# Two used-up phase places hold the transform constants of the last chunk's first four ticks

## The chip, the core and the metric

The kernel runs on one core of a Trainium2 chip. A core has a matrix engine (PE, which multiplies, with its weight loads PEld), a vector engine (DVE), a scalar engine (ACT), a general engine (POOL) and a sync engine (SP), each with its own queue of instructions, and 16 DMA engines that move data between the device memory and the on-chip memory. The metric is device time in microseconds (us) of one execution. Times of a profile count from the start of the profiled span.

## The reference

One layer over a sequence of 2048 positions with 640 features, all in float32. A vector `c` gives shifts, scales and gates (`mod`). A normalised, modulated copy of the input goes through a long convolution whose filter is the real part of a sum of 128 damped complex exponentials per feature; its gated result is added to the input, and a gated feed-forward part follows.

```python
h = _layernorm(x) * (1 + ca) + sa
# _A_ref, per feature d:
P = jnp.exp(logdA[:, :, None] * l[None, None, :])
K = jnp.einsum("dn,dnl,dn->dl", Cc, P, dB).real
Kf = rfft(pad(K)); Uf = rfft(pad(u))
y = irfft(Uf * Kf)[:L] + u * Dskip
x = x + ga * y
h = _layernorm(x) * (1 + cb) + sb
x = x + gb * ((silu(h @ w1) * (h @ w3)) @ w2)
```

## The kernel before

The convolution is done as a two-stage transform written as matmuls, over five chunks of 128 features (`NDC` = 5). For each chunk the filter's tables are made in eight steps of 16 features (`SD`), 40 steps in all: POOL makes integer phases (`phases`, tile `ph`, two steps at a time), ACT takes their cosine and sine in place, ACT makes exponentials (tables `A`), DVE multiplies (`E`, `A`), PE sums them (`kgen`) and does the filter's first stage (`k_stage1`), and `k_out` writes the result to `uk`.

The second stage works on groups. A chunk has eight groups of four frequencies, so there are 40 group steps, called ticks. Tick k, from 10 (`LAG`) to 49, belongs to chunk (k - 10) // 8 and group (k - 10) % 8; the last chunk has ticks 42 to 49. A tick runs these pieces, each a function of chunk and group:

- `stage2`: loads a constant tile `s2` (256 KB) with SP, unless one was loaded ahead and lies in the dictionary `ahead`; 16 matmuls multiply it with the input's and the filter's first stage in `uk` into the PSUM tile `p2`.
- `k_copy` (ACT, tile `kc`), `products` (DVE, tiles `T` and `p2` itself) and `sums` (DVE, tile `Y`) make the complex product.
- `inverse1`: loads a constant tile `i1` (256 KB) in the same way and runs 16 matmuls into `pz`. It comes one tick later than `stage2`, behind the next tick's `stage2`.
- `z_store`: ACT copies `pz` to `zt`, and a DMA writes it to the device memory (`zs`). For the last chunk `z_last` stores each group by itself, and behind groups 5 and 7 reloads the last columns.

`s2`, `i1`, `kc`, `T`, `Y` and `zt` are tiles of the pool `fp` with two places each. In the trace `s2` and `i1` have the names `s` and `i`, `p2` is `p`. A tile's load waits until the last reader of its place is done. The order of ACT, DVE and PE is written out by hand in the list `ROUND` as far as tick 42 (in a round that starts at 4 r, `iv+4` is `inverse1` of tick 4 r + 4); the loop over `tk` (line 981) does the rest. SP's instructions aren't pinned: the scheduler sets them in its own order, except where `tc.issue_after` puts one behind another on the same engine. `i1_last` (line 735) keeps the latest `i1` load for that.

In ticks 47 to 50 `x_part` (line 822) brings the first four row blocks back from `zs`, through loads that POOL issues (`z_load`, line 785), and DVE adds them to the input. Behind the last `i1` load go the first feed-forward weights (line 1001) and two blocks of the input. Then the pools of the convolution are closed and the feed-forward part begins with `x_first` (line 1050); it starts with matmuls on zeros (`idle`) that only keep PE busy.

A phase tile `ph` takes 8,576 bytes in each partition and the pool `tp` has three places for it. `tp` is closed at tick 41, and the pool `xp` of the feed-forward part is opened in its room. 20 phase tiles are made, the last for steps 38 and 39.

The lines behind which an `i1` or `s2` load stands are 685 and 691; those two names are also the key with which a tile is looked up in `ahead`.

Of the kernel before, what the change touches and what calls it, by code (L numbers as in the profile page):

```python
# [9 lines left out]
F32 = mybir.dt.float32  # L10
F32R = mybir.dt.float32r
I32 = mybir.dt.int32
# [5 lines left out]
P = 128  # L18
# [5 lines left out]
NDC = D // DC  # L24
SD = 16
# [9 lines left out]
NPG = NPH + NG - 1  # L35
# [57 lines left out]
def bc(ap, axis, n):  # L93
    v = ap.unsqueeze(axis)
    shape = list(v.shape)
    shape[axis] = n
    return v.broadcast_to(shape)
# [18 lines left out]
def tile_kernel(ctx: ExitStack, tc: tile.TileContext, a):  # L116
    nc = tc.nc
# [22 lines left out]
    def keep(ins):  # L140

        return tc.keep_in_program_order(ins) if in_order[0] else ins
# [22 lines left out]
    ssm = ExitStack()  # L165
# [7 lines left out]
    one4 = kp.tile([P, 1], F32, name="one4")  # L173
    cT = kp.tile([P, KD], F32, name="cT")
    uk = kp.tile([P, 3, NA, DC], F32, name="uk")

    psS = ssm.enter_context(tc.tile_pool(name="psS", bufs=1, space=PSUM))

# [2 lines left out]
    tp = tabs.enter_context(tc.tile_pool(name="tp", bufs=2, reuse_waits="tile"))  # L181
# [251 lines left out]
    def late_load(i):  # L433

        late[i] = w_load(xw[:, :KD * WC].rearrange("p (k c) -> p k c", k=KD), 1920 + i * WC)
# [108 lines left out]
    ph, cs, AA, EC, PK, K1 = {}, {}, {}, {}, {}, {}  # L544
# [39 lines left out]

    def phases(s):
        sl = slice(s * SD, s * SD + 2 * SD)
        p = tp.tile([P, 2 * SD, NPG], I32, name="ph", bufs=3)
        hold = tc.keep_in_program_order if 0 < s < 4 else keep
        b0 = NA - 8
        base = p[:, :, b0:NA]  # L590
        hold(G.tensor_tensor(p[:, :, b0:], bc(thi[:, sl], 2, NPG - b0), bc(iota, 1, 2 * SD), op=OP.mult))
        keep(G.tensor_tensor(base, base, bc(phi[:, sl], 2, 8), op=OP.add))
        keep(G.tensor_tensor(p[:, :, :b0].rearrange("p k (g j) -> p k g j", j=8), bc(base, 2, NG - 1),
                             bc(p[:, :, NPH:], 3, 8), op=OP.add))
        ph[s] = p[:, :, :NPH]
# [84 lines left out]
    ahead = {}  # L680
# [7 lines left out]
    def inverse1_load(g):  # L688

        i1 = fp.tile([P, 2, 2, P], F32, name="i1")  # L690
        i1_last[0] = nc.sync.dma_start(i1, a["i1"][:, g * 2:g * 2 + 2])
        return i1

    def stage2(ch, g):
        s2 = ahead.pop((ch, g, "s2"), None)
        if s2 is None:
            s2 = stage2_load(g)
        kn = 1 + ch % 2

        n = ch * 8 + g  # L700
        p2 = psS.tile([P, 2, 2, 2 * DC], F32, name="p2", tag="B" if n > NS - 12 and n % 2 else "A", bufs=1)
        for pi in range(2):
            for c in range(2):
                for par in range(2):
                    f = g * 4 + pi * 2 + par
                    keep(PE.matmul(p2[par * 64:par * 64 + 64, pi, c, :], s2[:, pi * 2 + par, c * 64:c * 64 + 64],
                                   uk[:, 0:kn + 1:kn, f, :], start=True, stop=True, tile_position=(0, par * 64)))
        Pq[ch, g] = p2
        if g % 2 == 1 and ch + 1 < NDC:
            u_load(ch + 1, g // 2)  # L710
# [24 lines left out]
    i1_last = [None]  # L735

    def inverse1(ch, g):
        i1 = ahead.pop((ch, g, "i1"), None)
        if i1 is None:
            i1 = inverse1_load(g)  # L740
        Y = Yq.pop((ch, g))
        if g % 2 == 0:
            Zq[ch] = psS.tile([P, 2, 4, DC], F32, name="pz", tag="Z", bufs=1)
        pz = Zq[ch]
        for pi in range(2):
            for c in range(2):
                for par in range(2):
                    r = slice(par * 64, par * 64 + 64)
                    ins = keep(PE.matmul(pz[:, par, (g % 2) * 2 + pi, :], i1[r, pi, c, :], Y[r, pi, c, :],
                                         start=(c == 0), stop=(c == 1), tile_position=(par * 64, 0)))  # L750
        return ins
# [33 lines left out]
    def z_load(z, j, ks, q=nc.sync, b0=0):  # L785

        nb = z.shape[1]
        for k in ks:
            hh = int(k > 1)
            kk = k - 2 * hh  # L790
            q.dma_start(z[hh * 64:hh * 64 + 64, :, kk * DC:kk * DC + DC],
                        zsv[:, 4 * j + b0:4 * j + b0 + nb, k])
# [7 lines left out]
    def z_tile():  # L800
        z = tz.tile([P, SD, 3, NA], F32, name="A")
        return z.rearrange("p k s b -> p (k s b)").rearrange("p (b d) -> p b d", b=4)
# [15 lines left out]
    def x_load(j):  # L818
        xe.append(xw[:, j * D:(j + 1) * D])
        nc.sync.dma_start(xe[j], a["x"][j * P:(j + 1) * P, :])  # L820
# [21 lines left out]
    def conv_part(fn):  # L842
        return lambda k: fn((k - LAG) // 8, (k - LAG) % 8)

    parts = {"PH": phases, "AB": absph, "CO": cosine, "SI": sine, "PA": lambda k: exp_fast((k,)), "XA": fast,
             "PQ": lambda k: exp_slow((k,)), "XQ": slow, "E1": real1, "E2": real2, "A1": imag1, "A2": imag2,
             "kg": kgen, "K": k1evac, "pt": k_stage1, "uk": k_out}
# [5 lines left out]
    def do(name, k):  # L853

        lo, hi = (LAG, LAG + 8 * NDC) if name in conv else (0, NS)
        if name in by_two and k % 2:
            return None
        if front[0]:
            assert (name, k) not in done and lo <= k < hi, (name, k)
        if (name, k) in done or not lo <= k < hi or (name == "zt" and k % 2 == 0 and k < LAG + 8 * NDC - 8):  # L860
            return None
        done.add((name, k))
        return (conv if name in conv else parts)[name](k)
# [20 lines left out]
    def u_first(i):  # L884

        u_load(0, i)
        if i == 0:
            ahead[0, 1, "s2"] = stage2_load(1)
            for g in range(2):
                ahead[0, g, "i1"] = inverse1_load(g)  # L890
# [45 lines left out]
    for word in FRONT:  # L936
        name, k = word[:2].rstrip("+"), int(word[len(word[:2].rstrip("+")):])
# [25 lines left out]
    for rnd in range(NS // EB):  # L963
        if 2 <= rnd < 7:
            late_load(rnd - 2)
        for word in ROUND:
            name, k = word[:2].rstrip("+-"), EB * rnd + int(word[len(word[:2].rstrip("+-")):])
            if name in pieces:
                if 2 <= rnd < 7:
                    pieces[name](rnd - 2)  # L970
                continue
            do(name, k)
            if name == "E1" and 30 <= k < 38 and k % 2 == 0:
                x_load((k - 30) // 2)

            if name == "kg" and 36 <= k < 40:
                early.append((None, z_tile()))
                z_load(early[-1][1], k - 36, range(3), q=nc.gpsimd)
    in_order[0] = False

    for tk in range(NS + 1, LAG + 8 * NDC + 2):
# [13 lines left out]
        i = tk - 1 - LAG - 8 * NDC + 8  # L995
# [190 lines left out]
    ahead = {(0, n): w for n, w in first_w.items()}  # L1186
# [272 lines left out]
    for pair in range(2):  # L1459
# [4 lines left out]
        side = []  # L1464
# [8 lines left out]
        if pair == 0:  # L1473
            tiles = []
            power = x_first(tiles)
            for k in range(KD):
# [12 lines left out]
            side = [lambda: mid(0), lambda: (mid(1), mid(2)), lambda: mid(3), lambda: None,  # L1489
                    lambda: turn(4, 0, 2), lambda: turn(3, 1)]  # L1490
# [106 lines left out]
```

## Time and profile before

| | |
|---|---|
| time, median of 3 runs | 943.76 us (942.69 to 943.88) |
| the profiled execution | 944.3 us, of which the span 942.3 us |
| PE busy | 874.9 us (93%) |
| DVE busy | 699.1 us (74%) |
| ACT busy | 541.6 us (57%) |
| POOL busy | 268.4 us (28%) |
| moved by DMA | 140.66 MB, 149 GB/s on average |
| first and last `stage2` | 123.5 and 360.9 us |
| loads of `s2` and of `i1` | 40 each, 256 KB, issued by SP |

The stretch that matters here lies between 300 us (tick 36) and 420 us (the feed-forward part under way). In the timeline a row has its start, its length, the engine, the line, the operation, output and input with their shapes, a count, and in brackets the idle time of the engine ahead of it with what ended it. Most instructions have line 110, that of the wrapper which records them, so they are told apart by their tiles. A row of PE with x16 and `p<-uk,s` is one tick's `stage2`, one with `pz<-Y,i` its `inverse1`. SPq rows are DMA issues; they show when a load was issued, not when it landed.

### The profile page before, as it was taken

The numbers are of one execution on the slowest core, as the hardware profiler recorded it, in microseconds if no ns is written. First come the engines' busy times: TensorE is split into PE (matmuls) and PEld (weight loads), VectorE is DVE, ScalarE is ACT, GpSimd is POOL, SyncE is SP. The second block draws the span as 40 slices with busy tenths as digits, with TensorE's granted clock in tenths as the row PEclk, the third lists the DMA queues.
The fourth block names the chain that finished last, engine by engine and source line by source line (L and its number), as shares of the span: only waits on it lengthen the run. The fifth ranks groups of instructions, "written<-read, shape, count | busy, mean of one in ns | idle before, by whom it ended". The sixth has DMA issues, their size and how long they took to land.

```text
span 942.3 us, 19918 instructions
## 1 busy us (share of the span) xinstructions
PE 874.9 (93%) x7950; PEld 665.5 (71%) x7950; DVE 699.1 (74%) x1209; ACT 541.6 (57%) x747; POOL 268.4 (28%) x277
## 2 busy tenths in 40 slices
PE   3788989999988888999999999999999999999997
PEld 2445566666666655678888886678888888888885
DVE  5899899999999857686666655677876666664674
ACT  6989889999999432474333322465643333323332
POOL 3333544554444011223222201320332222200341
PEclk9777689999999999999999999999999999999999
DMA  9664476576666786952111227946312322123352
GB/s 273 208 221 177 150 204 211 175 214 192 180 201 179 206 254 201 274 191 85 56 57 56 56 71 204 268 143 197 117 51 57 112 56 57 56 85 97 102 199 77
DMA packets 103279, 140.66 MB, mean 149 GB/s; under 512 B 20276, under 2 KB 62388, under 8 KB 103188
## 3 DMA queue, kind: packets, MB, share of 16 engines
q1 hardware_dynamic: 92452, 113.45, 39.8%
q10 hardware_dynamic: 8432, 18.22, 6.4%
q0 software_dynamic: 2304, 7.74, 2.5%
q8 instruction: 62, 1.02, 0.5%
q14 instruction: 29, 0.24, 0.1%
HBM read 107.92 MB, written 31.46 MB: 148 GB/s over the span
## 4 chain that ended last, share of the span: by engine, by line
PE 66%; DVE 15%; ACT 6%; DMA 5%; SPq 4%; issue 3%; POOL 0%; DVEq 0%; ACTq 0%; POOLq 0%
PE ps L110 49%; PE p L110 6%; SPq L110 3%; PE pt L110 3%; PE pz L110 3%; DVE A L110 2%; PE pk L110 2%; DVE E L110 2%; DVE u L110 2%; PE pa L110 2%; DVE uk L110 1%; DMA s<-in_s_dram 1%; DVE st L110 1%; ACT cs L110 1%; ACT A L110 1%
## 5 line engine op out<-in xcount | busy, mean ns | idle before, releaser
L110 DVE TENSOR_TENSOR s<-ps,s 128x512 f32<-128x512 f32 x138 | 94.9, 688 | 83.0 <-PE ps L110 82.7
L110 ACT CAST gh<-rw 128x640 fp32r<-128x640 f32 x87 | 63.3, 728 | 130.0 <-PE ps L110 90.8
L110 DVE TENSOR_TENSOR gl<-rw,gh 128x640 fp32r<-128x640 f32 x87 | 77.3, 888 | 71.1 <-ACT gh L110 71.1
L110 POOL TENSOR_TENSOR S<-rw 128x256 f32<-128x256 f32 x46 | 36.6, 797 | 234.7 <-DVE S0l L110 158.1
L110 PE MATMUL p<-uk,s 128*64 128x256 f32 x640 | 80.9, 396 | 15.1 <-DVE Y L110 3.4
L110 PE MATMUL ps<-xA,gh 128*128 128x512 f32 x280 | 87.6, 391 | 0.4 <-ACT xA L110 0.4
L110 PE MATMUL ps<-gh,uh 128*128 128x512 f32 x224 | 87.8, 392 | 0.0
L110 PE MATMUL ps<-gl,uh 128*128 128x512 f32 x224 | 87.4, 390 | 0.0
L110 POOL TENSOR_TENSOR ph<-thi,iota 128x1376 int32<-128x1376 int32 x20 | 51.2, 2560 | 115.8 <-DVE A L110 94.6
L110 DVE TENSOR_TENSOR E<-A,cs 128x1024 f32<-128x1024 f32 (+1 forms) x80 | 81.0, 1024 | 2.5 <-PE pk L110 1.9
L110 PE MATMUL ps<-gh,ul 128*128 128x512 f32 x208 | 81.1, 390 | 0.0
L110 PEld LDWEIGHTS p<-uk,s 128*64 128x64 f32 x640 | 46.3, 140 | 39.3 <-DVE Y L110 5.7
L110 ACT ACTIVATE A<-pa 128x1024 f32<-128x1024 f32 (+1 forms) x80 | 64.2, 814 | 9.4 <-PE pa L110 8.9
L110 PEld LDWEIGHTS ps<-xA,gh 128*128 128x128 f32 x280 | 52.3, 188 | 12.9 <-issue 1.2
L110 DVE TENSOR_TENSOR A<-A,ph 128x1024 f32<-128x1024 f32 x40 | 54.2, 1358 | 0.8
L110 PE MATMUL ps<-xA,gl 128*128 128x512 f32 x140 | 54.5, 389 | 0.0
L110 PE MATMUL pt<-s,K 128*64 128x128 f32 x640 | 46.8, 291 | 5.4 <-ACT uk L110 5.4
L110 PE MATMUL pz<-Y,i 64*128 64x128 f32 x640 | 46.9, 286 | 2.4 <-DVE Y L110 1.6
L110 PEld LDWEIGHTS ps<-gh,uh 128*128 128x128 f32 x224 | 42.2, 188 | 9.4 <-DVE h L110 0.6
L110 PEld LDWEIGHTS pz<-Y,i 64*128 64x128 f32 x640 | 39.3, 188 | 13.3 <-issue 8.9
L110 PEld LDWEIGHTS ps<-gl,uh 128*128 128x128 f32 x224 | 42.2, 188 | 9.0
L110 PEld LDWEIGHTS pt<-s,K 128*64 128x64 f32 x640 | 37.1, 145 | 14.1 <-ACT uk L110 8.7
(214 smaller groups left out, 2156.5 us busy)
## 6 DMA issues: line engine op xcount, KB each, us to landing
rw<-in_w_dram ACTq DMA_DIRECT2D x44, 320.0 KB
us<-u SPq DMA_DIRECT2D x16, 640.0 KB
s<-in_s_dram SPq DMA_DIRECT2D x40, 256.0 KB
i<-in_i_dram SPq DMA_DIRECT2D x40, 256.0 KB
rw<-in_wg_dram SPq DMA_DIRECT2D x31, 320.0 KB
rw<-in_wu_dram SPq DMA_DIRECT2D x28, 320.0 KB
uk<-us SPq DMA_DIRECT2D x16, 512.0 KB
zs<-zt SPq DMA_DIRECT2D x16, 512.0 KB
```

The lines of the kernel that those rows point to most:

```text
L110: ins = fn(*args, **kw)
```

## The change

The phase tiles get a pool of their own, `php`, with the same three places, on the side of the memory that stays until the convolution is over; so the phase places are no longer part of `tp`. After the `inverse1` of ticks 36, 37, 38 and 39 a new function `last_pair` loads the `s2` and the `i1` of the last chunk's groups 0, 1, 2 and 3 (ticks 42 to 45) and leaves them in `ahead`. Groups 0 and 1 share one phase tile, groups 2 and 3 the next; four constants of 512 floats each fill 8,192 of its 8,576 bytes in a partition. `tc.issue_after` puts each pair on SP behind the newest `i1` load. `stage2` and `inverse1` of ticks 42 to 45 then find their constants in `ahead` and take no place of `s2` and `i1` in `fp`. Ticks 46 to 49 load as before. The same bytes are loaded in all, and no computing instruction is added or left out.

```diff
--- before.py
+++ after.py
@@ -173,6 +173,10 @@
     one4 = kp.tile([P, 1], F32, name="one4")
     cT = kp.tile([P, KD], F32, name="cT")
     uk = kp.tile([P, 3, NA, DC], F32, name="uk")
+    php = ssm.enter_context(tc.tile_pool(name="php", bufs=3, side="right", reuse_waits="tile"))
+
+    def phase_tile():
+        return php.tile([P, 2 * SD, NPG], I32, name="ph")
 
     psS = ssm.enter_context(tc.tile_pool(name="psS", bufs=1, space=PSUM))
 
@@ -584,7 +588,7 @@
 
     def phases(s):
         sl = slice(s * SD, s * SD + 2 * SD)
-        p = tp.tile([P, 2 * SD, NPG], I32, name="ph", bufs=3)
+        p = phase_tile()
         hold = tc.keep_in_program_order if 0 < s < 4 else keep
         b0 = NA - 8
         base = p[:, :, b0:NA]
@@ -690,6 +694,19 @@
         i1 = fp.tile([P, 2, 2, P], F32, name="i1")
         i1_last[0] = nc.sync.dma_start(i1, a["i1"][:, g * 2:g * 2 + 2])
         return i1
+
+    kept = []
+
+    def last_pair(g):
+
+        if g % 2 == 0:
+            kept.append(phase_tile().rearrange("p k b -> p (k b)").bitcast(F32))
+        for i, (name, src, n) in enumerate((("s2", a["s2"], 4), ("i1", a["i1"], 2))):
+            o = (g % 2 * 2 + i) * 4 * P
+            v = kept[-1][:, o:o + 4 * P]
+            v = v.rearrange("p (f c) -> p f c", f=4) if i == 0 else v.rearrange("p (f h c) -> p f h c", f=2, h=2)
+            nc.sync.dma_start(v, src[:, g * n:g * n + n])
+            ahead[NDC - 1, g, name] = v
 
     def stage2(ch, g):
         s2 = ahead.pop((ch, g, "s2"), None)
@@ -970,6 +987,9 @@
                     pieces[name](rnd - 2)
                 continue
             do(name, k)
+            if name == "iv" and 36 <= k < 40:
+                with tc.issue_after(i1_last[0].ins):
+                    last_pair(k - 36)
             if name == "E1" and 30 <= k < 38 and k % 2 == 0:
                 x_load((k - 30) // 2)
 
```

## The prediction

> **What bounds the kernel now.** I read the page's chain first (DMA carries only 5% of it), then the chain in order of time, to see where that DMA sits. Between 300 and 370 us, in the last ticks of the convolution, two of its links are loads of the forward constant s2 (named `s<-in_s_dram`), and each has matmuls waiting at its end. In the chain of waits the columns are start, length and what:
>
> ```profile
> 332.02 6.59 DMA s<-in_s_dram
> ...
> 338.75 3.25 PE p L110 x16
> ...
> 345.33 5.39 DMA s<-in_s_dram
> ```
>
> The same stretch in the timeline of PE. `p<-uk,s` is `stage2` of a tick (16 matmuls), `pz<-Y,i` is `inverse1` of the tick before. Counting back from the last one (tick 49), the row at 338.75 is `stage2` of tick 43, 343.35 tick 44, 346.31 tick 45, 350.77 tick 46, 353.74 tick 47, 357.30 tick 48.
>
> ```profile
> 335.28 1.16 PE L110 MATMUL pz<-Y,i 64*128 64x128 f32 x16
> 338.75 3.25 PE L110 MATMUL p<-uk,s 128*64 128x256 f32 x16 [2.31 <-DMA s<-in_s_dram]
> 341.93 1.48 PE L110 MATMUL pz<-Y,i 64*128 64x128 f32 x16
> 343.35 1.95 PE L110 MATMUL p<-uk,s 128*64 128x256 f32 x16
> ...
> 346.31 1.95 PE L110 MATMUL p<-uk,s 128*64 128x256 f32 x16
> 349.12 1.16 PE L110 MATMUL pz<-Y,i 64*128 64x128 f32 x16 [0.85 <-DMA i<-in_i_dram]
> 350.77 1.95 PE L110 MATMUL p<-uk,s 128*64 128x256 f32 x16 [0.49 <-DMA s<-in_s_dram]
> ...
> 353.74 1.95 PE L110 MATMUL p<-uk,s 128*64 128x256 f32 x16
> ...
> 357.30 1.95 PE L110 MATMUL p<-uk,s 128*64 128x256 f32 x16
> ```
>
> An undisturbed tick is 346.31 - 343.35 = 2.96 us. Three stalls on constants stand in these rows: 2.31, 0.85 and 0.49 us. The first has an aftermath: tick 43 takes 3.25 us where the others take 1.95, and the inverse behind it 1.48 where the others take 1.16. The table by windows tells why. Its columns are PE, PEld, DVE, ACT and POOL busy, then the granted clock, the DMA share and GB/s:
>
> ```profile
> 335.00:340.00 5.00, 2.69 (x28) 1.93 (x26) 2.14 (x4) 1.60 (x2) 0.00 (x0) 0.92 0.99 355
> 340.00:345.00 5.00, 5.00 (x42) 3.25 (x38) 2.14 (x4) 1.17 (x2) 2.44 (x4) 0.74 0.38 116
> ```
>
> The stall lies where the DMA share is 0.99, and behind it the granted clock falls to 0.74. So ticks 43 to 46 are bound by their constants, twice directly and once through the clock.
>
> **The change, part by part.** Every load of a constant goes into one of two places, so the load for tick k waits until tick k-2 has used the place. SyncE's timeline shows it:
>
> ```profile
> 300.31 0.33 SPq L691 DMA_DIRECT2D i<-in_i_dram  x1
> ...
> 309.54 0.53 SPq L685 DMA_DIRECT2D s<-in_s_dram  x1
> 312.21 0.33 SPq L691 DMA_DIRECT2D i<-in_i_dram  x1
> ...
> 316.81 0.33 SPq L691 DMA_DIRECT2D i<-in_i_dram  x1
> ...
> 321.22 0.58 SPq L685 DMA_DIRECT2D s<-in_s_dram  x1
> ...
> 328.58 0.33 SPq L685 DMA_DIRECT2D s<-in_s_dram  x1
> ...
> 342.03 0.33 SPq L685 DMA_DIRECT2D s<-in_s_dram  x1
> ```
>
> The load at 342.03 goes out as tick 43 ends (338.75 + 3.25 = 342.0), and tick 45 at 346.31 uses it without a wait: it landed within 4.28 us. The one at 345.33 took 5.39. I keep these two as the ends for a load's time.
>
> *The eight moved loads.* The s2 and i1 of ticks 42 to 45 (256 KB each) now go out behind the i1 loads of ticks 36 to 39, the first at 300.31 and the last at 316.81. They need two phase places. The last readers of those are DVE's `A<-ph` of tables 35 and 37:
>
> ```profile
> 298.87 0.69 DVE L110 SCALAR_TENSOR_TENSOR A<-ph,A 128x512 f32<-128x512 f32 x1
> ...
> 310.00 0.69 DVE L110 SCALAR_TENSOR_TENSOR A<-ph,A 128x512 f32<-128x512 f32 x1
> ```
>
> Table 35 ends at 299.56, ahead of the first pair (300.31). Table 37 ends at 310.69, ahead of the i1 load of tick 38 (312.21), behind which the pair that takes its place stands. So the new waits cost nothing, and nothing is held up behind them on SP. SP pays eight issues of 0.33 us in a stretch where it mostly waits.
>
> *The rotation skips four ticks.* The next load through the rotation is that of tick 46, and its place is free once tick 40 is done (the 328.58 issue marks that moment). Ticks 46 and 47 thus find theirs loaded long before.
>
> *The sum.* The stalls go: 2.31 + 0.85 + 0.49 = 3.65. The slow aftermath goes with the first: 3.25 - 1.95 = 1.30, and 1.48 - 1.16 = 0.32. Together 5.27 us. A check by the timeline: PE is done with tick 41's inverse at 335.28 + 1.16 = 336.4; four ticks of 2.96 bring tick 47 to 348.2, against 353.74: 5.5 us. I keep 5.3.
>
> *What is late next.* Tick 48's load waits for tick 46, which then ends at 336.4 + 3 x 2.96 + 1.95 = 347.2, and lands 4.28 to 5.39 us later, at 351.5 to 352.6. PE reaches tick 48 no sooner than 357.30 - 353.74 = 3.56 after tick 47 (`x_part`'s matmuls lie between), at 351.8. The loss is 0 to 0.8 us. I take 0.2, near the short end, because the loads of ticks 46 and 47 that crowded this stretch are then done. Further on DVE sets the pace already:
>
> ```profile
> 356.35 0.69 DVE L110 TENSOR_TENSOR T<-p,kc 128x512 f32<-128x512 f32 x1 [0.76 <-ACT kc L110]
> ...
> 359.92 0.68 DVE L110 TENSOR_TENSOR T<-p,kc 128x512 f32<-128x512 f32 x1
> ```
>
> One tick of DVE with `x_part`'s additions is 3.57 us, the same before and after, and it starts from tick 47. So the shift of tick 47 carries to tick 49. `x_part`'s matmuls need the z loads issued by POOL (the second row is from the list of DMA issues; its last column is the median time to landing):
>
> ```profile
> 342.46 2.44 POOL L791 DMA_DIRECT2D A<-zs  x4 [9.34 <-DMA zs<-zt]
> ```
>
> ```profile
> A<-zs POOLq DMA_DIRECT2D x16, 128.0 KB, 4.8
> ```
>
> They don't move: the last goes out by 344.9 and lands near 349.7. The first `x_part` comes just ahead of tick 48, after 350, so its data is there and I cost it at nothing.
>
> *What follows tick 49.* The stores of z, the reloads and the first weights hang on the last ticks:
>
> ```profile
> 361.00 0.33 ACTq L110 DMA_DIRECT2D zs<-zt  x1
> ...
> 366.54 4.64 POOL L779 DMA_DIRECT2D A<-zs  x8 [21.64 <-DMA xm<-in_x_dram]
> ...
> 369.86 1.32 SPq L779 DMA_DIRECT2D A<-zs  x4
> ```
>
> All are issued behind tick 47 or 49 and shift with them. One new squeeze: zt has two places, and at 2.96 us a tick a store has 2 x 2.96 - 0.6 = 5.3 us to land before ScalarE reuses its place, with the next kc copy queued behind. The store at 361.00 landed at the latest at 366.54, 5.5 us on. So 0 to 0.2 us a pair of ticks; I take 0.
>
> Net gain 5.3 - 0.2 = 5.1 us, between 4.4 and 5.7. The profiled execution took 944.3 us (a span of 942.3 and 2.0 around it), so 939.2 by it; the median of the runs shown, 943.76, is 0.5 lower, so **938.7** by the median.
>
> **The rivals.** *1. The rotation's loads come late (941.4).* Nothing pins the loads of ticks 46 and 47 to an early spot in SP's order. If SP reaches tick 46's only as tick 44 ends (341.4 after the shift), it lands 5.39 later and tick 46 loses 1.4 us; if only as tick 45 ends, 4.4 us. The middle is 2.9 of 5.3, and leaves 2.4. Against it: in the rows above every load goes out at the moment its place comes free.
>
> *2. Given back behind (943.5).* The stage after the convolution is limited by loads:
>
> ```profile
> 390.00:395.00 5.00, 5.00 (x35) 3.38 (x34) 3.57 (x7) 2.78 (x4) 0.24 (x1) 1.00 1.19 203
> ```
>
> If these loads, or the order in which ACT, DVE and SP take their work there, kept their old times, the whole gain would be absorbed. Against it: they are issued behind 369.86, which shifts, and PE is busy throughout this window.
>
> *3. Slower: the pairs delay the current chunk (946.7).* The DMA rows where the pairs go are nearly full, and these are the uses of the constants loaded at 309.54 and 321.22:
>
> ```profile
> 305.00:310.00 5.00, 4.02 (x98) 2.72 (x94) 4.90 (x9) 4.91 (x5) 0.83 (x2) 1.00 0.91 278
> 310.00:315.00 5.00, 3.44 (x48) 2.88 (x46) 4.49 (x10) 3.27 (x4) 1.83 (x3) 1.00 0.98 257
> 315.00:320.00 5.00, 5.00 (x115) 3.82 (x113) 4.61 (x9) 2.09 (x3) 0.00 (x0) 1.00 0.61 169
> ```
>
> ```profile
> 318.76 1.95 PE L110 MATMUL p<-uk,s 128*64 128x256 f32 x16
> ...
> 329.56 1.95 PE L110 MATMUL p<-uk,s 128*64 128x256 f32 x16
> ```
>
> A pair is 512 KB: 2.0 us at 257 GB/s, 8.2 us for four. Tick 39 has 318.76 - 309.54 = 9.2 us for its load and tick 41 has 8.3; with a landing of 6.59 that leaves 2.6 and 1.7 us. If nothing of the pairs had drained when these loads go out, tick 39 would stall 4.1 - 2.6 = 1.5 us and tick 41 8.2 - 1.7 = 6.5 us. That is 8.0 us against the gain of 5.1: 2.9 us slower, 946.7. It turns the sign from a backlog of 5.3 us at 321.22 on. Against it: the share falls to 0.61 from 315 to 320, and the pairs spread over 16 us.
> The Trainium skill ("DMA: Bandwidth & Descriptors", Queues, rings and completion order) says that each DMA engine consumes a queue's descriptors in ring order: by that rule a pair ahead of a needed load does delay it, by its whole transfer. The rows above show share, not order.
>
> *4. The second slow stretch moves (939.5).* The clock falls once more, to 0.50, over the matmuls that only keep PE busy:
>
> ```profile
> 370.00:372.00 2.00, 2.00 (x6) 1.52 (x6) 0.44 (x3) 0.24 (x1) 1.19 (x3) 0.50 0.49 126
> ```
>
> ```profile
> 369.81 4.11 PE L110 MATMUL ps<-idle 128*128 128x512 f32 x10 [0.98 <-DVE xm L110]
> ...
> 375.71 4.40 PE L110 MATMUL ps<-idle 128*128 128x512 f32 x18
> 380.74 2.67 PE L110 MATMUL ps<-ident,T 128*128 128x128 f32 x20 [0.62 <-ACT T L110]
> ```
>
> Ten take 0.41 us each, the eighteen 0.244. The first slow stretch, at the same half speed, was 5 x (0.08 + 0.26) x 2 = 3.4 us long (from 0.92 and 0.74). One of that length on the eighteen would cost 3.4 x (1 - 0.244/0.41) = 1.4 us, of which 0.62 is covered: 0.8 lost. The Trainium skill ("TensorE: Matmul & The Clock Gate", Part 1) says that the clock is judged in a free-running window of 3413 ns, which doesn't shift with the program; by it a program that shifts by 5.1 us meets the grid elsewhere. The trace agrees in so far as the clock fell only behind stretches with gaps.
>
> **How the numbers follow.** Forecast 0.62, rival 1 0.10, rival 2 0.12, rival 3 0.08, rival 4 0.08. About 0.2% (1.9 us) is what a measurement here can tell from no change. Faster: 0.62 + 0.10 + 0.08 = 0.80; same 0.12; slower 0.08. The range covers the forecast's 4.4 to 5.7 with the half microsecond that the runs scatter (937.7 at the low end) and rivals 1 and 4, up to 942.0; it leaves out 2 and 3, 0.20.
>
> **What would show it.** Right: eight more SP issues between 300 and 318; no DMA wait of `p<-uk,s` in ticks 43 to 47; a clock of 1.00 from 335 to 345; tick 47 near 348.3, and `pz` of tick 49 near 360.4 instead of 365.45. Wrong: new waits on `s` between 313 and 330 (rival 3); the load for tick 46 issued after 340 (rival 1); an equal shift at 366 that is gone by 411 (rival 2).

## The result and the profile after

| | before | after |
|---|---|---|
| median of 18 runs each | 945.4 us | 940.19 us |
| lowest and highest | 942.08 to 949.89 us | 937.38 to 943.51 us |
| span of the profiled execution | 942.3 us | 938.2 us |
| ratio after / before | | 0.9947, 95% interval 0.9933 to 0.9962 |

The ratio is 5.0 us on 945.4, with an interval of 3.6 to 6.3 us. The forecast was a gain of 5.1; its 938.7 us started from 943.76, the median of the first three runs, and over 18 runs the kernel before has 945.4. The last ticks, in the timeline of PE after the change (`p<-uk,ph` and `pz<-Y,ph` read a constant from a phase place):

```profile
334.15 1.95 PE L110 MATMUL p<-uk,ph 128*64 128x256 f32 x16
336.03 1.16 PE L110 MATMUL pz<-Y,i 64*128 64x128 f32 x16
337.12 1.95 PE L110 MATMUL p<-uk,ph 128*64 128x256 f32 x16
339.00 1.16 PE L110 MATMUL pz<-Y,ph 64*128 64x128 f32 x16
...
346.03 1.95 PE L110 MATMUL p<-uk,s 128*64 128x256 f32 x16
347.91 1.16 PE L110 MATMUL pz<-Y,ph 64*128 64x128 f32 x16
349.00 1.95 PE L110 MATMUL p<-uk,s 128*64 128x256 f32 x16
```

Ticks 42 (334.15) to 47 (349.00) follow each other in steps of 2.97 us with nothing in brackets: no wait on a constant, and no tick of 3.25 us. The windows over the same stretch show the clock at full grant where it was 0.92 and 0.74:

```profile
335.00:340.00 5.00, 5.00 (x60) 3.43 (x54) 2.54 (x6) 2.18 (x3) 0.00 (x0) 1.00 0.90 299
340.00:345.00 5.00, 5.00 (x54) 3.15 (x50) 4.07 (x8) 1.76 (x3) 1.79 (x3) 1.00 0.39 137
```

Two rows speak against a clean gain. The first stands earlier on PE. Tick 39, which had no wait before, now has one on its own constant, and the chain in order of time shows that constant's load at 9.40 us:

```profile
319.49 1.95 PE L110 MATMUL p<-uk,s 128*64 128x256 f32 x16 [0.84 <-DMA s<-in_s_dram]
```

```profile
310.05 9.40 DMA s<-in_s_dram
```

The second loss lies behind tick 49. PE's timeline from its inverse on:

```profile
360.72 1.22 PE L110 MATMUL pz<-Y,i 64*128 64x128 f32 x16 [1.55 <-DVE Y L110]
...
365.07 2.53 PE L110 MATMUL ps<-idle 128*128 128x512 f32 x10 [0.98 <-DVE xm L110]
369.97 2.08 PE L110 MATMUL ps<-A,i 64*32 64x128 f32 x32 [2.36 <-DMA A<-zs]
371.98 6.55 PE L110 MATMUL ps<-idle 128*128 128x512 f32 x18
378.37 2.35 PE L110 MATMUL ps<-ident,T 128*128 128x128 f32 x20
```

```profile
370.00:375.00 5.00, 5.00 (x39) 3.32 (x40) 2.28 (x12) 0.00 (x0) 0.45 (x2) 0.50 0.38 112
```

Tick 49's inverse comes 4.73 us earlier (360.72 against 365.45; 0.18 of it was there at tick 36 already), but the first transpose behind it only 2.37 us earlier (378.37 against 380.74). In between the first ten idle matmuls run at full clock (2.53 instead of 4.11 us), PE then stands for 2.36 us, and the clock falls to half over the eighteen that follow: 6.55 us instead of 4.40. This execution gets a part of it back later: the same rows of PE lie 2.75 us apart at 390.90 in before and 388.15 in after, 3.31 at 584.77 and 581.46, 3.62 at 609.97 and 606.35, and the span is 4.1 us shorter. In before the clock falls once more, to 0.84 from 585 to 590 us and 0.82 from 590 to 595, where after has 1.00; but from 584.77 to 609.97 the distance grows by 0.3 us only.

```profile
585.00:590.00 5.00, 3.31 (x21) 1.18 (x20) 3.32 (x7) 2.07 (x3) 0.12 (x1) 0.84 0.89 253
590.00:595.00 5.00, 5.00 (x19) 4.05 (x20) 2.57 (x5) 2.08 (x3) 1.58 (x5) 0.82 0.72 213
```

### The profile page after: what moved, and what is told of

Same layout as the page of the kernel before. It is cut to its first block, busy times and chain, and to the rows that moved or that the text cites. A ratio compares the mean times of both kernels' runs of the same rounds, so it can differ in the third digit from the quotient of the medians.

```text
span 938.2 us, 19912 instructions
## 1 busy us (share of the span) xinstructions
PE 872.8 (93%) x7950; PEld 664.4 (71%) x7950; DVE 698.8 (74%) x1209; ACT 541.4 (58%) x747; POOL 268.5 (29%) x277
## 4 chain that ended last, share of the span: by engine, by line
PE 65%; DVE 13%; ACT 7%; DMA 6%; SPq 4%; issue 4%; POOL 0%; DVEq 0%; ACTq 0%; POOLq 0%
PE ps L110 49%; PE p L110 6%; SPq L110 4%; PE pz L110 3%; PE pt L110 3%; PE pk L110 2%; DVE A L110 2%; DVE u L110 2%; PE pa L110 2%; DVE E L110 2%; DVE uk L110 1%; DMA A<-zs 1%; DVE st L110 1%; DMA s<-in_s_dram 1%; ACT A L110 1%
## 5 line engine op out<-in xcount | busy, mean ns | idle before, releaser
L110 PE MATMUL p<-uk,s 128*64 128x256 f32 x576 | 71.8, 392 | 13.1 <-DVE Y L110 3.3
L110 PEld LDWEIGHTS p<-uk,s 128*64 128x64 f32 x576 | 41.3, 139 | 34.9 <-DVE Y L110 5.7
L110 POOL TENSOR_TENSOR ph<-ph 128x768 int32<-128x768 int32 x20 | 45.0, 2248 | 1.6
L110 POOL TENSOR_TENSOR rw<-rw,gbr 128x512 f32<-128x512 f32 x14 | 20.6, 1472 | 86.1 <-DMA rw<-in_w_dram 82.9
```

The lines of the kernel that those rows point to most:

```text
L110: ins = fn(*args, **kw)
```

## The experiments

A profile's times count from the start of the span, and the start of tick 36 lies anywhere from 300.7 to 304.9 us in these profiles (302.48 and 304.87 in late_idle18 and late_pairs, which are the same kernel up to there). So the runs are compared by two distances on PE: from the start of tick 36's `stage2` to the start of tick 49's `inverse1` (in before 365.45 - 302.13 = 63.32), and from there to the first transpose (380.74 - 365.45 = 15.29). Both can be read from the timeline of one execution. The times of whole runs scatter by several us, so most intervals below are too wide to rank the variants among themselves. Each ratio is to runs of the kernel before that were taken along with it (their medians are 942.1 to 945.4), so the medians of two rows aren't to be compared.

| run | wait at tick 39 | tick 36 to 49 | 49 to transpose | median, us | ratio to before, 95% |
|---|---|---|---|---|---|
| before | 0 | 63.32 | 15.29 | | |
| after | 0.84 | 58.77 | 17.65 | 940.19 | 0.9947 [0.9933, 0.9962] |
| after_again | 1.62 | 59.52 | 15.42 | 937.23 | 0.9933 [0.9908, 0.9957] |
| layout_only | 0 | 63.81 | 16.86 | 943.79 | 0.9998 [0.9975, 1.0021] |
| late_pairs | 0 | 57.82 | 14.70 | 938.76 | 0.995 [0.9926, 0.9975] |
| late_again | 0 | 57.83 | 16.25 | 937.78 | 0.9922 [0.9898, 0.9947] |
| late_idle18 | 0 | 57.83 | 16.31 | 939.97 | 0.9947 [0.9923, 0.9972] |
| after_idle18 | 1.12 | 59.02 | 14.68 | 940.18 | 0.9953 [0.9936, 0.997] |
| one_place | 1.10 | 59.94 | 17.76 | 939.44 | 0.9952 [0.9931, 0.9972] |
| s2_only | 0 | 58.98 | 14.80 | 937.66 | 0.9925 [0.9898, 0.9952] |
| double_37 | 2.99 | 62.51 | 15.06 | 941.84, one run | |
| pool_pairs | 5.36 | 65.85 | 15.53 | 945.48 | 1.0031 [1.0004, 1.0057] |
| pool_first | 2.31 | 61.33 | 14.68 | 943.53, one run | |

### The control: after_again

The changed kernel once more.

> The changed kernel once more, as control and as a second sample of the matrix engine's clock. Theory 1 (what ends at tick 49 is fixed by waits, and only the slow stretch of the clock behind it lies where it happens to lie): tick 49's inverse again near 360.7 us and tick 39's forward matmuls again about 0.8 us late on their constant; the length and place of the slow stretch after 365 us may differ from the 6.8 us of the first profile. Rival (the slow stretch belongs to the program): again 6.8 us from 369.8, and the eighteen idle matmuls again 6.5 us. Time ratio to the kernel before 0.9947 by both, about 5.0 us.

Tick 39 waits 1.62 us this time, and tick 49 is 0.75 us later than in the first profile (59.52 against 58.77), which is that wait's difference (0.78). The slow stretch was shorter: the ten idle matmuls again at full clock, then three small waits on `A<-zs` instead of one of 2.36 us, and the eighteen in 5.63 us.

```profile
365.69 2.56 PE L110 MATMUL ps<-idle 128*128 128x512 f32 x10 [0.98 <-DVE xm L110]
...
371.29 5.63 PE L110 MATMUL ps<-idle 128*128 128x512 f32 x18
```

The wait at tick 39 belongs to the change, though its size varies; the length of the slow stretch isn't fixed by the program.

### Only the pool: layout_only

```diff
-            if name == "iv" and 36 <= k < 40:
-                with tc.issue_after(i1_last[0].ins):
-                    last_pair(k - 36)
```

> The phase tiles in their own pool as in the change, but no pair is loaded ahead. Theory 1 (the gain is the loads' alone): as the kernel before, ratio 1.000, the wait of 2.3 us on s2 at tick 43 and the inverse of tick 49 near 365.4. Rival (part of the gain comes from the other places of the pools behind the convolution or from the scheduler's order there): faster by 1 us or more, or a tick 49 that ends as before and a feed-forward part that starts sooner after it.

The ratio is 0.9998, and the distance to tick 49 isn't shorter than before: moving the phase places by itself brings nothing that shows (the interval of the whole runs would let up to 2.4 us pass). The waits are spread another way than in the profile of before, tick 43 (340.22) and tick 46 (352.01):

```profile
340.22 1.95 PE L110 MATMUL p<-uk,s 128*64 128x256 f32 x16 [1.41 <-DMA s<-in_s_dram]
342.10 1.16 PE L110 MATMUL pz<-Y,i 64*128 64x128 f32 x16
...
352.01 2.96 PE L110 MATMUL p<-uk,s 128*64 128x256 f32 x16 [2.81 <-DMA s<-in_s_dram]
354.90 1.77 PE L110 MATMUL pz<-Y,i 64*128 64x128 f32 x16
```

Here tick 46 has the long wait and the slow matmuls behind it, and tick 43 a wait without them. The sum is 1.41 + 2.81 + (2.96 - 1.95) + (1.77 - 1.16) = 5.84 us, against 5.27 in before. So the cost is that of the rotation as a whole and not of one tick, and it was there in both executions; which tick has the long wait differs.

### The pairs two ticks later: late_pairs and late_again

```diff
-            if name == "iv" and 36 <= k < 40:
+            if name == "iv" and 38 <= k < 42:
                 with tc.issue_after(i1_last[0].ins):
-                    last_pair(k - 36)
+                    last_pair(k - 38)
```

> The four pairs stand behind the i1 loads of ticks 38 to 41 instead of 36 to 39. Theory 1 (the pairs at ticks 36 and 37 sit ahead of tick 39's constant, whose load took 9.4 us): that load lands within 7 us, tick 39 starts without a wait on it, and all that follows to tick 49 comes about 0.8 us earlier (inverse of tick 49 near 359.9), with ticks 42 to 47 still free of waits on constants. Rival (tick 39 was late for another reason, or pairs two ticks later only push the same delay onto tick 41 or 42): the wait of 0.8 us stays or turns up at ticks 41 to 43, inverse of tick 49 at 360.7 or later.

> late_pairs once more, on the same chip as the three others. Theory 1: again no wait on tick 39's constant and 57.8 us from tick 36's forward matmuls to tick 49's inverse; the place of the slow stretch differs from run to run, so from there to the first transpose 14.7 to 17.7 us. Rival (the missing wait at tick 39 was luck of one execution): a wait of 0.8 us or more there.

Tick 39 starts without a wait in both, and the distance to tick 49 is 57.82 and 57.83 us, the same to 0.01. In late_pairs tick 39 and tick 42 read:

```profile
321.48 1.95 PE L110 MATMUL p<-uk,s 128*64 128x256 f32 x16
...
336.13 1.95 PE L110 MATMUL p<-uk,ph 128*64 128x256 f32 x16
```

Nothing was pushed onto ticks 41 to 43. This is the stretch with no wait on a constant at all, and it gives the full worth of the loads: 63.32 - 57.83 = 5.5 us, the prediction's check by the timeline to the tenth. (Against layout_only's 63.81 it is 6.0, so the tenth is luck.) The change as made gets 4.55 and 3.8 of it. With 57.83 as the base the other rows add up: after 57.83 + 0.84 = 58.67 (58.77 measured), after_again 59.45 (59.52), before 57.83 + 5.27 = 63.10 (63.32). By whole times late_pairs isn't shown to beat the change: 0.995 and 0.9922 with intervals that overlap 0.9947 and 0.9933.

### One place instead of two: one_place

```diff
-            if name == "iv" and 36 <= k < 40:
+            if name == "iv" and 36 <= k < 38:
```

> Only the first phase place is used: the constants of ticks 42 and 43, behind the i1 loads of ticks 36 and 37; ticks 44 to 49 use the rotation. Theory 1 (what costs is the one late load of tick 43 and the clock that falls behind it, and a rotation that has skipped two ticks stays ahead): no wait at tick 43, ticks 44 and 45 loaded before 340, tick 46 late by 0 to 1.4 us, the inverse of tick 49 at 360.7 to 362.1, ratio 0.995 to 0.996. Rival (each tick loaded ahead brings its own share, so half the ticks bring half): about 2.5 us of the 5, inverse of tick 49 near 363, ratio 0.9973.

Ticks 43, 44 and 45 have no wait; tick 47 has one of 0.86 us, since the rotation's lead is used up two ticks sooner (a late tick 46 was expected):

```profile
350.40 1.95 PE L110 MATMUL p<-uk,s 128*64 128x256 f32 x16 [0.86 <-DMA s<-in_s_dram]
```

Less the wait at tick 39, which it shares with the change, one_place loses 0.86 us and 0.15 of small waits of the 5.5. Half the constants bring four fifths: in this execution most of the worth comes from the rotation getting ahead at all. And the wait at tick 39 is there with the first two pairs alone, so the two that go out behind tick 39's constant don't add to it.

### Only the forward constants: s2_only

```diff
-        for i, (name, src, n) in enumerate((("s2", a["s2"], 4), ("i1", a["i1"], 2))):
+        for i, (name, src, n) in enumerate((("s2", a["s2"], 4),)):
```

> Only the s2 of ticks 42 to 45 is loaded ahead; their i1 keeps the rotation of two places. Theory 1 (the forward constant of tick 43 and, in some runs, of tick 46 is what PE waits for, with the clock that falls behind it; i1 costs 0.85 us at most): from the start of tick 36's forward matmuls to the start of tick 49's inverse 58.8 to 60 us (63.3 before, 58.8 with the whole change), waits on i1 of up to 1 us at ticks 42 to 45. Since only half the bytes go ahead, tick 39's wait on its own constant shrinks from 0.8 to 1.6 us to less than 0.8. Rival (both constants of a tick are equally late, so i1 takes the place of s2 as the wait): waits on i1 of 1.5 us or more at ticks 43 to 45 and that distance above 61 us.

The inverse constants stay in the rotation and cost two waits of 0.27 us, not 1.5. With half the bytes ahead of it, tick 39 has no wait at all. The distance is 58.98, so as good as the change; about 0.6 us of it over 57.83 isn't in these waits, and 0.5 of that lies in one block of matmuls into `pt` (the filter's first stage) that took 1.58 instead of 1.09 us. The clock was at 1.00 there, and the rows don't tell the cause:

```profile
322.01 1.58 PE L110 MATMUL pt<-s,K 128*64 128x128 f32 x16 [0.69 <-ACT uk L110]
```

### Doubling what stands ahead of tick 39: double_37

```diff
-            if name == "iv" and 36 <= k < 40:
+            if name == "iv" and 37 <= k < 40:
                 with tc.issue_after(i1_last[0].ins):
-                    last_pair(k - 36)
+                    for g in ((0, 1), (2,), (3,))[k - 37]:
+                        last_pair(g)
```

> The pair of tick 36 moves to tick 37, so two pairs (1 MB) instead of one stand ahead of tick 39's constant on SP. Theory 1 (what delays that constant is the transfer of what was issued ahead of it on the same queue): the wait at tick 39 grows from 0.84 to 1.62 us by about 512 KB at 257 GB/s, 2.0 us, to 2.6 to 3.7 us, and tick 49's inverse comes later by the same, 60.5 to 61.8 us behind the start of tick 36's forward matmuls (58.8 and 59.5 with the change as it is). Rival (the delay is that of the pair's order on SP or of a full stretch of DMA that one pair more doesn't change): 0.8 to 1.6 us again.

The wait grew to 2.99 us, inside the expected 2.6 to 3.7, and the clock falls behind it: tick 39 takes 3.36 us.

```profile
321.14 3.36 PE L110 MATMUL p<-uk,s 128*64 128x256 f32 x16 [2.99 <-DMA s<-in_s_dram]
```

With that aftermath (1.41 us) the distance came to 62.51, 0.7 above the upper end that was expected. So what stands right ahead of tick 39's constant on SP is the cause of its delay. But the size doesn't come from the bytes alone, as theory 1 had it. SyncE's timeline and the chain:

```profile
308.82 0.70 SPq L708 DMA_DIRECT2D ph<-in_i_dram  x1
309.57 0.64 SPq L708 DMA_DIRECT2D ph<-in_s_dram  x1
310.25 0.45 SPq L708 DMA_DIRECT2D ph<-in_i_dram  x1
310.74 0.48 SPq L689 DMA_DIRECT2D s<-in_s_dram  x1
```

```profile
310.74 10.36 DMA s<-in_s_dram
```

SP issues one load after the other, so the constant goes out 9.28 us behind the start of tick 36's `stage2` (310.74 - 301.46), where after, whose first pair went out at 300.56 already, has 8.10 and before 7.41. Of the 2.15 us by which the wait grew over after's, 1.18 is this later issue, and 0.96 the longer load (10.36 instead of 9.40).

### The same loads from another queue: pool_pairs and pool_first

```diff
-            nc.sync.dma_start(v, src[:, g * n:g * n + n])
+            nc.gpsimd.dma_start(v, src[:, g * n:g * n + n])
```

> The pairs are issued by POOL, among its loads of z, and no longer by SP; SP's queue is that of the kernel before without the constants of ticks 42 to 45. The bytes and roughly the moment stay (the first place is free at about 299.6 us, the second at 310.7). Theory 1 (the delay of tick 39's constant comes from standing behind the pairs on SP's queue): that load lands in less than 8.5 us, tick 39 has no wait on it or one below 0.3 us, and from tick 36's forward matmuls to tick 49's inverse 57.8 to 58.2 us. Rival (the DMA engines' share is what counts, whoever issues): a wait of 0.8 us or more at tick 39 again.

That theory fell. Off SP's queue the pairs did worse: tick 39 waits 5.36 us, its load takes 14.61 us, the clock falls behind it, and the kernel is slower than before (1.0031). In pool_pairs, the chain and PE's timeline:

```profile
309.48 14.61 DMA s<-in_s_dram
```

```profile
324.13 3.68 PE L110 MATMUL p<-uk,s 128*64 128x256 f32 x16 [5.36 <-DMA s<-in_s_dram]
```

POOL's timeline shows when they went out: two pairs (the s2 and i1 of two ticks) by 304.9 and two more by 315, around the issue of tick 39's constant (309.48):

```profile
302.67 0.58 POOL L708 DMA_DIRECT2D ph<-in_s_dram  x1
...
311.16 0.56 POOL L708 DMA_DIRECT2D ph<-in_s_dram  x1
...
314.40 0.55 POOL L708 DMA_DIRECT2D ph<-in_i_dram  x1 [0.27 <-DMA A<-zs]
```

A new theory: only the later two pairs hurt, which on SP would have stood behind that constant. pool_first has the first two alone (`36 <= k < 38` with the edit above).

> As pool_pairs, but only the first phase place: the constants of ticks 42 and 43, issued by POOL at about 303 to 305 us; ticks 44 and 45 use the rotation. Theory 1 (the wait of 5.36 us at tick 39 came from the two later pairs, which POOL issued while tick 39's constant was on its way and which on SP's queue would have stood behind it): the wait falls to 1 us or less. Rival (each pair that POOL issues ahead delays that constant alike): about half of 5.36, 2 to 3.5 us.

It fell as well: 2.31 us, nearly half of 5.36, as the rival had it.

```profile
323.74 1.95 PE L110 MATMUL p<-uk,s 128*64 128x256 f32 x16 [2.31 <-DMA s<-in_s_dram]
```

The waits count only what is left when the constant's margin is used up. The load itself, and the moment of its issue behind the start of tick 36's `stage2`, tell more:

| run | pairs that go out ahead of it, and by whom | issue behind tick 36 | load | wait |
|---|---|---|---|---|
| before | none | 7.41 | at most 9.22 | 0 |
| after | two, SP | 8.10 | 9.40 | 0.84 |
| one_place | two, SP | 8.21 | 9.54 | 1.10 |
| double_37 | two, SP, right ahead | 9.28 | 10.36 | 2.99 |
| pool_first | two, POOL | 7.40 | 11.56 | 2.31 |
| pool_pairs | two, POOL, and two more while it is under way | 7.39 | 14.61 | 5.36 |

```profile
310.39 9.54 DMA s<-in_s_dram
```

```profile
312.14 11.56 DMA s<-in_s_dram
```

The first line is from the chain of one_place, the second from that of pool_first. With SP the pairs delay the issue by 0.7 to 1.9 us and lengthen the load; with POOL the constant goes out on time, and its load is longer by at least 2.3 us with two pairs and 5.4 with all four. So the transfers themselves hold it up, whoever issues them. The Trainium skill says so too ("DMA: Bandwidth & Descriptors", Issuing engines are not separate DMA queues): DMAs of the scalar, sync and general engine run on the same 16 DMA engines and interleave, and issuing from several saves only issue time. These runs agree: another queue saved the 0.7 us of the issue and gave no relief beyond. Why the load takes 2.0 us longer beside POOL's two pairs than behind SP's stays open. The moments aren't the same, and POOL's own loads of z go out later too (in pool_pairs four of them from 304.84 on, where before has five from 302.76 on).

### More idle matmuls: after_idle18 and late_idle18

```diff
-    IDLE = (10, 18)
+    IDLE = (18, 18)
```

> The changed kernel with eighteen instead of ten matmuls on zeros ahead of x_first's first products. Theory 1 (behind tick 49 PE stands idle for about 2.4 us once ten matmuls at full clock take 2.5 us, and that gap is what lets the clock fall over the next eighteen): no gap over 0.7 us between the first idle matmuls and the products, no slow stretch between 366 and 380, the second eighteen in 4.4 us, and from the start of tick 49's inverse to the first transpose 15.0 us or less (17.65 and 15.4 us in the two profiles of the change, 15.3 before). Rival (the clock falls for the gaps of 1.55, 0.57 and 0.98 us ahead of the idle matmuls, wherever the grid lies): a slow stretch there again, now over more idle matmuls, and that distance 17 us or more.

> Both: pairs behind the i1 loads of ticks 38 to 41 and eighteen idle matmuls. Theory 1 (the two losses are separate and both go): no wait on tick 39's constant, from tick 36's forward matmuls to tick 49's inverse 57.8 us, from there to the first transpose 15.0 us or less; ratio to the kernel before 0.993 or lower, the lowest of the series. Rival (loads behind tick 49 end the wait in any case, so the idle matmuls don't matter): ratio as with late_pairs alone, 0.995.

In after_idle18 PE has no gap ahead of the products and the clock never falls there; the distance to the first transpose is 14.68 us:

```profile
365.37 4.36 PE L110 MATMUL ps<-idle 128*128 128x512 f32 x18 [0.98 <-DVE xm L110]
369.66 1.08 PE L110 MATMUL ps<-A,i 64*32 64x128 f32 x32
370.67 4.42 PE L110 MATMUL ps<-idle 128*128 128x512 f32 x18
```

In late_idle18 it fell all the same, now over the first eighteen, which made the products late (16.31 us):

```profile
364.66 5.98 PE L110 MATMUL ps<-idle 128*128 128x512 f32 x18 [0.98 <-DVE xm L110]
```

Neither theory holds alone. The gap of 2.36 us isn't needed for a slow stretch; those of 1.55, 0.57 and 0.98 us in front can be enough, and late_pairs and pool_first, with ten idle matmuls, had none (14.70 and 14.68). So the 14.68 of after_idle18 can't be put down to its edit. Over the profiles of this study the distance is 14.7 to 17.8 us whatever the variant. The best whole time was not reached by this edit: 0.9953 and 0.9947, where 0.993 or lower was expected of late_idle18.

## Why the prediction was right, point by point

- **The sum at ticks 43 to 47.** It was right, and in its better form: the stalls added up to 5.27, the timeline to 5.5, and late_pairs measures 5.5. The slow matmuls belonged in the sum; layout_only pays them at another tick. That tick 43 had the long wait was chance (in layout_only it is tick 46); that the rotation is late shows in both.
- **Ticks 46 and 47 find their constants loaded.** Shown: after has no wait there. Rival 1 didn't come up.
- **Tick 48's load, costed at 0.2 us (0 to 0.8).** It cost nothing: tick 48 starts 3.56 us after tick 47 (352.56 and 349.00), as before. Its load went out as tick 46 ended, by SyncE's timeline at 348.02, and so landed within 4.54 us, near the short end as expected.

```profile
348.02 0.33 SPq L689 DMA_DIRECT2D s<-in_s_dram  x1
```

- **DVE's 3.57 us with `x_part`, zt's two places, the z loads.** No new wait: DVE's additions follow each other as before, and tick 49's inverse waits the same 1.55 us on `Y`.
- **"The new waits cost nothing, and nothing is held up behind them on SP."** This step failed, not through the waits for a place but through what the pairs do to the load behind them. Tick 39's constant came late by 0.84 us in one profile and 1.62 in another, which is the sign of being wrong that the prediction gave for rival 3 (new waits on `s` between 313 and 330). Part of it is order: of tick 37's pair the i1 went out only at 309.31, right in front of tick 39's constant, and not at once behind the s2, so that constant's issue moved from 7.41 to 8.10 us behind tick 36. The price of an issue on SP was counted (eight of 0.33 us), but as if it fell where nothing was due.

```profile
305.95 0.42 SPq L708 DMA_DIRECT2D ph<-in_s_dram  x1
306.62 0.33 SPq L782 DMA_DIRECT2D zs<-zt  x1
308.88 0.38 SPq L682 DMA_DIRECT2D uk<-us  x1
309.31 0.69 SPq L708 DMA_DIRECT2D ph<-in_i_dram  x1
310.05 0.42 SPq L689 DMA_DIRECT2D s<-in_s_dram  x1
```

- **Rival 3.** The mechanism was right, its all-or-nothing price wasn't. Its two terms fared differently: 1.5 us for tick 39, where 0.84 to 1.62 came in all four runs with whole pairs behind ticks 36 and 37 on SP (after, after_again, after_idle18, one_place), and 6.5 for tick 41, which waited in none of them. So the first term belonged in the forecast, and the chance of 0.08 should have gone to the second alone. double_37 and pool_pairs show how much further it can go, and pool_pairs passes the point from which the change is a loss: 5.36 us of wait and 3.68 - 1.95 = 1.73 of slow matmuls, more than the 5.5 gained.
- **Rival 4.** Right in kind, too small in size: 0.8 us expected, 17.65 - 15.29 = 2.36 lost up to the first transpose in the profile of after. Two things were missed. The slow stretch can last twice as long (the clock was at 0.50 from 370 through 375, and the eighteen took 6.55 us instead of 4.40). And with the ten idle matmuls at full clock PE waits for the reloads of z, which in this execution came later than before: the products start 9.25 us behind the inverse (369.97 - 360.72), before 8.40 (373.85 - 365.45). The Trainium skill's free-running window ("TensorE: Matmul & The Clock Gate", Part 1) fits what the runs show: late_pairs and late_again, the same program, have the same distance to tick 49 to 0.01 us, and yet differ by 1.55 us behind it. The window itself is shown by no run here.
- **Rival 2.** Not seen: PE's rows behind the slow stretch stay 2.75 us apart at 390.90 and 3.31 at 584.77, so the stage behind absorbed nothing. The clock's fall at 585 us in before brought 0.3 of the profile's 4.1 us, and late_pairs has a fall there too.

So at tick 49 the forecast of 5.1 was 0.4 short of what the loads are worth (5.5) and missed the 0.9 to 1.7 that tick 39 takes back: 4.55 and 3.8 us in the two profiles. The whole runs give 5.0 us, and their interval (3.6 to 6.3) holds these too. What lies behind tick 49 adds or takes a few us by the place of the slow stretch, in before as well; whether that averages out over the whole runs isn't shown. So the mechanism of the gain is shown, and that 5.1 and 5.0 agree to a tenth is luck: a gain that was taken too low and a loss at tick 39 that was taken as nothing offset each other in part.

## What to carry to other kernels

A load moved ahead isn't free because its place is: look up which loads go out in the moments after its new place, how much time each has until its use, how full the DMA engines are there, and how much later the queue issues them, then put the move where that margin is widest (here two ticks later). A rotation of two places that is just too slow can be cured by letting it skip a few turns, and half the skipped turns brought most of the gain. A stall of PE costs more than its length where the clock falls behind it (it doesn't always), so count the slow matmuls with it, and don't compare two profiles behind such a stretch without looking at the clock first.

## What wasn't expected of the hardware

- A load of 256 KB at whose end PE waited took from 4.75 us (one_place, tick 47, by the chain) to 14.61 us (pool_pairs, tick 39), by what else was under way.
- The same 1 MB made tick 39 wait 1.10 us when SP issued it, 0.8 us of which is a later issue of its constant, and 2.31 us when POOL did, with the issue on time.
- A wait of 2.31 us on PE let the clock fall in before (tick 43 took 3.25 us) and not in pool_first (tick 39 took 1.95).
- Idle time of PE of 1.55, 0.57 and 0.98 us within 7 us was followed by a slow stretch over the very next idle matmuls in before, layout_only and late_idle18 and not in the others; of the same program, late_pairs had none up to the first transpose and late_again had one over the eighteen idle matmuls. A slow stretch covered 3.4 us or about twice that.
